# Loads, norms and fill work moved in the head of an attention and mixer kernel: channel weights in two late pieces, norms of pairs 6 to 8 ahead of the drain, rest rows last, more channel work in slots 6 to 8

## The chip, the cores and the metric

The kernel runs on one core of one Trainium2 chip. The metric is device time in microseconds (us). A profiled run gives a span that is about 1.8 us shorter than the run's own time (418.8 and 417.0 us for the kernel before).

The engines are called TensorE (PE in the profile; PEld is its weight load), VectorE (DVE), ScalarE (ACT), GpSimd (POOL) and SyncE (SP). In the traces each works through its own instructions in the order in which the kernel gives them.

## The reference

Cosine attention, then an MLP mixer over tokens and channels. All inputs and the output are float32; the kernel computes in float16 with float32 sums.

```python
# q, k, v: (8, 12, 448, 64); tau = 0.1
q_n = q / (norm(q, axis=-1) + 1e-6);  k_n = k / (norm(k, axis=-1) + 1e-6)
attn = softmax(q_n @ k_n.T / tau)
x = (attn @ v), heads side by side                 # (8, 448, 768)
xt = x.transpose(0, 2, 1)
u = x + (relu(xt @ w_tok1) @ w_tok2).transpose(0, 2, 1)      # token MLP, 448 -> 256 -> 448
out = u + relu(u @ w_ch1) @ w_ch2                            # channel MLP, 768 -> 1536 -> 768
```

## The kernel before

Two heads make a pair; there are 48 pairs, 6 for each batch. The order of instructions is written by hand in slots: slot i computes the scores of pair i, and beside them the values of pair i-1, the token MLP of pair i-2 and, from slot 6 on, some channel MLP of a finished batch. Slot 6 is special: it finishes the token MLP of pairs 4 and 5, the last two of the first batch (the "drain"), after which the first channel matmul can start. Three pairs make a half, which is the unit of loading and of the norms' tile of 45 columns (9 for the rest rows, 12 for each pair). The 448 rows are 3 blocks of 128 and 64 "rest rows". To get a pair ready takes a chain over four engines: squares (ScalarE, GpSimd), sums (VectorE), 1/norm by logarithms and exponentials (ScalarE), scaling to `kq` (GpSimd), transposes (TensorE) and a copy to `qk` (VectorE).

```python
def cast_v(n):                       # values of half n to float16
    (nc.vector if n < 3 else nc.gpsimd).tensor_copy(out=vts[n % NV]..., in_=vm[n]...)
    # ... rest rows of the values, GpSimd

def busy(n):                         # matmuls of the identity: keep TensorE active
    w = ps.tile([P, 512], FP32, name=f"busy_{n}", tag="b")
    for _ in range(n): nc.tensor.matmul(w..., id16[:], ..., start=True, stop=True)

def pv(p, a):                        # two row blocks of attn @ v
    # ...
    for mm in range(2):
        lo = P * (2 * a + mm)
        nc.tensor.matmul(psO[:, mm, :], pt[:, PX + lo:PX + lo + P], vx[:, j, 0:2 * E1], start=True, stop=False)   # rest rows
        for g in range(2):
            for c in range(NC):
                nc.tensor.matmul(psO[:, mm, E1 * g:E1 * (g + 1)], pt[:, at:at + P], vt[:, 2 * j + g, c, 0:E1],
                                 start=False, stop=(g == 1 and c == NC - 1))
    # ... reciprocal and x = psO * rec, VectorE

# --- tables: in which slot ---
early_sq = {3: 0, 4: 1, 5: 1, 6: 4, 7: 5, 8: 5, 9: 6, ...}            # squares of a pair
sum_at = at({p: s + 1 for p, s in sq_slot.items()})                    # sums one slot later
sc_at = at({p: {6: 5, 7: 6}.get(p, ...)})                              # scaling
cast_at = at({n: {1: 2, 2: 5}.get(n, 3 * n - 2) for n in range(1, NHALF)})

# --- before slot 0 ---
busy(26)
# ... squares, sums, norms of pair 0; scaled(0, nc.vector); rnorms(0, 0, 9)
sums(1)
scaled_x(0, nc.vector, 0, 1)         # pair 0's rest rows
rnorms(0, 21, 33)                    # pair 1's norms, ScalarE
# ...

# --- slot i ---
if i == FIRST:                       # FIRST = 6
    pv(i - 1, 0); m_tok1(i - 2); pv(i - 1, 1); next_qk(i); tok2(i - 2)
    m_tok1(i - 1); score(i, 0); tok2(i - 1); score(i, 1); feed(0.0, 3000.0)     # feed: channel units
elif i < NP_ALL:
    score(i, 0); score(i, 1)
# ... norm_sums, rnorms, norm_begin (squares), norm_scale by the tables
if i == 0:
    weights_ch1(0); weights_ch1(1)   # first channel weights, 2 x 1152 KB, issued by GpSimd
if i in (5, 6):
    weights_ch2(i - 5)               # second channel weights, 2 x 1152 KB
# ... values, scores of the rest, next pair's transposes, token MLP, channel units by quota
```

## Time and profile before

| | before |
|---|---|
| time, median of 3 runs (range) | 418.96 us (416.81 to 419.09) |
| span of the profiled run | 417.0 us |
| TensorE busy | 393.3 us, 94% |
| sum of TensorE's waits that the profile lists | 18.3 us, about 17 of them before 77 us |
| clock granted to TensorE | below 1.00 in most of 10 to 70 us, then 1.00 |

The table by stretches shows where TensorE is not full. The columns are the stretch, its length, then the busy time of PE, PEld, DVE, ACT and POOL (with instructions), the granted clock of TensorE, the share of the transfer engines, and GB/s.

```profile
10.00:20.00 10.00, 5.31 (x35) 2.62 (x35) 6.08 (x9) 7.26 (x17) 9.51 (x16) 0.63 1.15 260
20.00:30.00 10.00, 7.93 (x98) 5.32 (x96) 8.19 (x18) 8.62 (x19) 9.71 (x14) 0.86 1.19 225
30.00:40.00 10.00, 9.45 (x137) 6.76 (x136) 7.99 (x19) 7.29 (x11) 3.21 (x5) 1.00 1.14 230
40.00:50.00 10.00, 7.09 (x88) 5.52 (x84) 6.28 (x17) 4.05 (x9) 6.37 (x10) 0.83 1.19 276
50.00:60.00 10.00, 6.71 (x41) 3.15 (x40) 3.43 (x5) 6.36 (x13) 4.58 (x7) 0.84 1.25 224
60.00:70.00 10.00, 9.00 (x85) 4.91 (x83) 6.04 (x13) 7.58 (x18) 7.51 (x12) 0.81 1.10 214
70.00:80.00 10.00, 8.81 (x99) 5.43 (x99) 5.03 (x11) 6.98 (x14) 10.00 (x14) 1.00 0.92 211
```

A stretch with a granted clock below 1.00 is called cold here. From 80 to 400 us TensorE is busy 318.7 of 320 us at clock 1.00. The list of TensorE's waits names what it waited for (total us, times, longest):

```profile
PE psU L319 <- DVE r L303: 4.0, 4, 2.6
PE pst L240 <- DVE kq L218: 2.7, 1, 2.7
PE pst L240 <- POOL kq L207: 2.5, 2, 2.1
PE psS L259 <- DVE qk L245: 2.3, 3, 0.8
PE psS L259 <- ACT pt L260: 2.2, 6, 0.6
...
PE psG L347 <- DVE qk L245: 1.2, 1, 1.2
```

The longest wait of the first line, 2.6 us, is not slow VectorE work. VectorE's timeline around 41 us (start, duration, instruction, and in brackets the idle time before it and what ended it) shows the cast of the third half's values waiting for its load, and pair 3's relu `r` standing behind it in order. GpSimd's own wait for the rest keys of pair 6 is of the same kind: their load was late.

```profile
41.36 0.76 DVE L164 CAST vt<-vm 128x1152 f16<-128x1152 f32 x1 [1.14 <-DMA vm<-in_v_dram]
42.04 0.18 DVE L285 RECIPROCAL rec<-psO 128x4 f32<-128x4 f32 x1
42.25 0.42 DVE L286 TENSOR_TENSOR x<-psO,rec 128x256 f16<-128x256 f32 x1
42.59 0.41 DVE L303 TENSOR_SCALAR r<-psR 128x256 f16<-128x256 f32 x1
```

```profile
38.93 0.51 POOL L176 TENSOR_TENSOR sqx<-xk 128x192 f32<-128x192 f32 x1 [6.79 <-DMA xk<-in_k_dram]
...
55.42 0.82 POOL L207 TENSOR_TENSOR kq<-km,rn 128x384 f16<-128x384 f32 x1 [8.36 <-ACT rn L200]
```

The last of these lines is the second hole: GpSimd idles 8.36 us until ScalarE delivers norms, while TensorE waits for `kq` (the 2.5 us of the list):

```profile
56.30 0.34 PE L240 MATMUL pst<-id,kq 128*128 128x128 f16 x3 [2.09 <-POOL kq L207]
```

### The profile page before, as it was taken

The page shows a single profiled execution, that of the slowest core. Times are in us where ns is not written, and L with a number is a line of the kernel's source. Part 1 is how long each engine was busy: PE and PEld are TensorE (multiplying, and loading weights), DVE is VectorE, ACT ScalarE, POOL GpSimd, SP SyncE. Part 2 cuts the span into 40 slices and gives each one's busy share as a digit, 9 for nine tenths or more (in the row PEclk, how much of TensorE's full clock was granted, in tenths as well). Part 3 has the DMA queues.
Part 4 walks back from the last instruction along what each step waited for, and adds up shares of the span by engine and source line. Part 5 has one row for each costly group of instructions (what it writes and reads, how often), then busy time and mean ns, then how long its engine had stood idle before and what let it go on. Part 6 is the DMA issues. An engine that isn't in the chain of part 4 may idle for free.

```text
span 417.0 us, 9079 instructions
## 1 busy us (share of the span) xinstructions
PE 393.3 (94%) x3638; PEld 229.5 (55%) x3638; DVE 203.3 (49%) x456; ACT 225.6 (54%) x401; POOL 219.1 (53%) x321
## 2 busy tenths in 40 slices
PE   7588869899999999999999999999999999999995
PEld 3255634566655655555555655555555565565562
DVE  5687734657545464536553645446553443243021
ACT  4797367665376645674566445764576435521400
POOL 4993459999349293929392855839391600000000
PEclk9599879999999999999999999999999999999999
DMA  8999999946997396989897399989992353013012
GB/s 222 258 220 232 287 212 203 227 82 179 213 190 138 75 243 170 248 136 240 179 248 142 88 222 169 238 140 232 187 190 49 85 146 64 14 31 124 2 75 76
DMA packets 137162, 67.51 MB, mean 162 GB/s; under 512 B 93152, under 2 KB 133536, under 8 KB 137120
## 3 DMA queue, kind: packets, MB, share of 16 engines
q1 hardware_dynamic: 132800, 61.46, 68.6%
q0 software_dynamic: 3632, 5.18, 6.9%
q8 instruction: 28, 0.46, 0.5%
q10 hardware_dynamic: 688, 0.30, 0.2%
q14 instruction: 14, 0.11, 0.1%
HBM read 43.38 MB, written 11.01 MB: 130 GB/s over the span
## 4 chain that ended last, share of the span: by engine, by line
PE 79%; POOL 5%; DMA 4%; issue 4%; DVE 3%; ACT 2%; POOLq 0%
PE psF L361 25%; PE psG L347 24%; PE psO L281 7%; PE psS L259 7%; DMA vm<-in_v_dram 4%; PE psR L300 4%; PE psU L319 4%; PE psX L266 3%; PE psO L277 3%; POOL kq L207 2%; POOL sq L176 2%; POOL sqx L176 1%; ACT pt L260 1%; PE psU L324 1%; POOL kq L218 1%
## 5 line engine op out<-in xcount | busy, mean ns | idle before, releaser
L260 ACT ACTIVATE pt<-psS 128x896 f16<-128x896 f32 x144 | 126.5, 915 | 82.0 <-PE psS L259 81.9
L347 PE MATMUL psG<-ut,wc1t 128*128 128x448 f16 x576 | 123.3, 355 | 1.8 <-DVE qk L245 1.2
L361 PE MATMUL psF<-wc2t,gt 128*128 128x384 f16 x672 | 117.1, 326 | 0.0
L349 ACT ACTIVATE gt<-psG 128x448 f16<-128x448 f32 x96 | 52.3, 544 | 75.1 <-PE psG L347 75.0
L207 POOL TENSOR_TENSOR kq<-km,rn 128x384 f16<-128x384 f32 x47 | 39.6, 843 | 94.9 <-ACT rn L200 93.6
L361 PEld LDWEIGHTS <-gt 128*128 128x128 f16 x672 | 63.1, 98 | 41.3 <-issue 3.3
L347 PEld LDWEIGHTS <-wc1t 128*128 128x128 f16 x576 | 52.4, 98 | 49.6 <-issue 7.9
L364 DVE TENSOR_TENSOR ost<-psF,ur 128x384 f32<-128x384 f32 x56 | 31.2, 557 | 78.4 <-PE psF L361 75.0
L281 PE MATMUL psO<-vt,pt 128*128 128x65 f16 x1152 | 59.2, 196 | 0.0
L281 PEld LDWEIGHTS <-pt 128*128 128x128 f16 x1152 | 52.4, 99 | 5.2
L189 DVE TENSOR_REDUCE ssq<-sq 128x12 f32<-128x768 f32 x48 | 45.1, 948 | 14.3 <-POOL sq L176 14.2
L259 PE MATMUL psS<-qk 64*128 64x448 f16 x288 | 46.1, 367 | 4.7 <-DVE qk L245 2.3
L277 PE MATMUL psO<-vx,pt 128*128 128x130 f16 x192 | 43.0, 224 | 0.1
L286 DVE TENSOR_TENSOR x<-psO,rec 128x256 f16<-128x256 f32 x96 | 40.7, 424 | 3.3
L176 POOL TENSOR_TENSOR sq<-km 128x384 f32<-128x384 f32 x47 | 39.0, 833 | 5.4 <-DMA km<-in_k_dram 5.3
L285 DVE RECIPROCAL rec<-psO 128x4 f32<-128x4 f32 x96 | 17.1, 179 | 49.9 <-PE psO L281 49.6
L207 POOL TENSOR_TENSOR kq<-qm,rn 128x384 f16<-128x384 f32 x47 | 38.9, 827 | 0.0
L329 DVE TENSOR_TENSOR ut<-psU,xT 128x448 f16<-128x448 f32 (+2 forms) x39 | 17.6, 478 | 26.9 <-PE psU L319 18.3
L176 POOL TENSOR_TENSOR sq<-qm 128x384 f32<-128x384 f32 x36 | 29.6, 823 | 1.3 <-POOL kq L218 0.5
L319 PE MATMUL psU<-w2t,r 128*128 128x448 f16 x96 | 26.2, 356 | 4.1 <-DVE r L303 4.0
L300 PE MATMUL psR<-x,w1t 128*128 128x128 f16 x384 | 29.6, 221 | 0.0
L259 PEld LDWEIGHTS <-qk 64*128 64x128 f16 x288 | 11.0, 94 | 32.7 <-issue 27.4
(61 smaller groups left out, 327.9 us busy)
## 6 DMA issues: line engine op xcount, KB each, us to landing
vm<-in_v_dram SPq DMA_DIRECT2D x16, 576.0 KB, 7.4
out_dram<-ost SPq DMA_DIRECT2D x24, 384.0 KB, 2.7
qm<-in_q_dram SPq DMA_DIRECT2D x15, 576.0 KB, 5.1
km<-in_k_dram SPq DMA_DIRECT2D x15, 576.0 KB, 7.1
wc1t<-in_moe_w_ch_dram POOLq DMA_DIRECT2D x2, 1152.0 KB, 16.8
wc2t<-in_moe_w_ch_dram POOLq DMA_DIRECT2D x2, 1152.0 KB, 12.8
out_dram<-ost SPq DMA_DIRECT2D x8, 192.0 KB, 2.8
xq<-in_q_dram SPq DMA_DIRECT2D x7, 192.0 KB, 8.0
```

The lines of the kernel that those rows point to most:

```text
L176: eng.tensor_tensor(out=out, in0=src, in1=src, op=ALU.mult)
L189: nc.vector.tensor_reduce(out=ssqs[p // HP % 3][:, lo:lo + 12], in_=sq[p][:].rearrange("p a g e -> p (a g) e"), axis=AXX.X, op=ALU.add)
L207: eng.tensor_tensor(out=kqs[n % 2][:, j, a, 0:NC, :].rearrange("p c (g e) -> p g c e", g=2), in0=src, in1=_bcast_free(rn, E), op=ALU.mult)
L259: nc.tensor.matmul(psS[:, g, 0:S], qk[r, P * c:P * (c + 1)], qk[r, 512:512 + S], start=True, stop=True)
L260: nc.scalar.activation(out=pt[:, 2 * S * c:2 * S * (c + 1)].rearrange("p (g s) -> p g s", g=2), in_=psS[:, :, 0:S], func=AF.Exp, scale=inv ...
L277: nc.tensor.matmul(psO[:, mm, :], pt[:, PX + lo:PX + lo + P], vx[:, j, 0:2 * E1], start=True, stop=False)
L281: nc.tensor.matmul(psO[:, mm, E1 * g:E1 * (g + 1)], pt[:, at:at + P], vt[:, 2 * j + g, c, 0:E1], start=False, stop=(g == 1 and c == NC - 1))
L300: nc.tensor.matmul(psR[:, tt, :], w1t[:, m, tt * P:(tt + 1) * P], xs[p][:, m, :], start=(m == 0), stop=(m == NC))
L319: nc.tensor.matmul(psU[:], rs[p][:, tt, :], w2t[:, tt, lo:lo + S], start=(tt == 0), stop=by_dma and tt == TT - 1)
L347: nc.tensor.matmul(psG[:], wc1t[:, dt, ct * P:(ct + 1) * P], ut[:, dt, sp], start=(dt == 0), stop=(dt == DT - 1))
L349: nc.scalar.activation(out=gt[:, ct, sp], in_=psG[:], func=AF.Relu)
L361: nc.tensor.matmul(psF[:], gt[:, ct, lo:lo + P], wc2t[:, ct, dh * DH:(dh + 1) * DH], start=(ct == 0), stop=(ct == CT - 1))
```

## The change

Its intent: let the third half's loads pass before the channel weights; get pairs 6 to 8 scaled before the drain, so that the pairs behind it are ready; keep the clock up with more dummy matmuls; hand out channel work sooner. The diff, cut:

```diff
 def cast_v(n):
-    (nc.vector if n < 3 else nc.gpsimd).tensor_copy(...)
+    (nc.vector if n < 2 else nc.gpsimd).tensor_copy(...)
 # busy() may write into any tile; 4 more dummies inside pair 0's transposes, 2 before
 # the first score of slots 0 to 3
+            if p == 0 and (a, c) == (0, NC):
+                busy(w, 4)
+        busy(psS[:, 0, :], fill)                         # in score(p, c, fill=0)
 # pv: rest rows last
-            nc.tensor.matmul(psO[:, mm, :], pt[:, PX + lo:PX + lo + P], vx[:, j, 0:2 * E1], start=True, stop=False)
...
-                                     start=False, stop=(g == 1 and c == NC - 1))
+                                     start=(g == 0 and c == 0), stop=False)
+            nc.tensor.matmul(psO[:, mm, :], pt[:, PX + lo:PX + lo + P], vx[:, j, 0:2 * E1], start=False, stop=True)
 # tables
-    early_sq = {3: 0, 4: 1, 5: 1, 6: 4, 7: 5, 8: 5, ...
+    early_sq = {3: 0, 4: 1, 5: 1, 6: 3, 7: 4, 8: 5, ...
-    sum_at = at({p: s + 1 for p, s in sq_slot.items()})
+    sum_at = at({p: s + (p != 8) for p, s in sq_slot.items()})
     # one norm call for all 45 columns of half 2, at the end of slot 5
-    sc_at = at({p: {6: 5, 7: 6}.get(p, ...
+    sc_at = at({p: {6: 5, 7: 5}.get(p, ...
-    cast_at = at({n: {1: 2, 2: 5}.get(...
+    cast_at = at({n: {1: 2, 2: 6}.get(...
 # before slot 0
+        scaled_x(0, nc.vector, 0, 1)
         sums(1)
-        scaled_x(0, nc.vector, 0, 1)
 # slots
-            quota = max(sum(t for t, _ in queue) - 2000.0, 0.0) / left
+            quota = max(...) / (4 if FIRST <= i < FIRST + 3 else left)
     # slot 6: both value halves, tok1(4), tok2(4), tok1(5), tok2(5), 2 us of channel work,
     # then transposes of pair 6, its scores, 2 us of channel work
-                norm_begin(p, nc.scalar if p < 12 else nc.gpsimd, nc.gpsimd)
+                norm_begin(p, nc.scalar if p < 18 else nc.gpsimd, nc.gpsimd)
-            if i == 0:
-                weights_ch1(0)
-                weights_ch1(1)
+            if i in (2, 4):
+                weights_ch1(i // 4)
-            if i in (5, 6):
-                weights_ch2(i - 5)
+            if i in (6, 7):
+                weights_ch2(i - 6)
     # end of slot 5
+                if i == FIRST - 1:
+                    norm_sums(8)
+                    norm_rn()
+                    for p in sc_at[i]:
+                        norm_scale(p, nc.gpsimd)
```

## The prediction

> **What bounds the kernel now.** TensorE is busy 393.3 of 417.0 us (the page). By stretches it is full at clock 1.00 from 80 to 400 us; almost all loss lies in the first 77 us. There the waits of TensorE add up to about 16 us: 2.7 us for the first rest rows (VectorE, until 12.4), 2.6 us until 43.1 (relu queued in VectorE's order behind the value cast, whose load landed at 41.4), about 3.3 us around 56 to 58 us for pair 6's scaled q and k (GpSimd behind the norms), and many small ones. After each gap of 2 us or more the clock drops: seven transposes take 0.93 to 0.95 us at 16, 21 and 59 us but 0.55 us at 30 us. The Trainium skill, "TensorE: Matmul & The Clock Gate", Part 1, says an idle TensorE falls back to half clock until it has been busy a while; the trace agrees. Three cold stretches (12 to 23, 43 to 46.5, 56 to 63.7 us) cost an estimated 8 us.
>
> The loads are bandwidth bound: GB/s by stretch is 220 to 260 from 0 to 60 us. The two channel pieces, issued at 19.8 and 20.6 us (1152 KB each), stand in front of the third half's keys and values.
>
> **What changes.**
> 1. First-layer channel weights are issued in slots 2 and 4: 1.7 us of GpSimd issue leaves the busy start, and 2.4 MB leaves the way of half 2. Its rest keys (landed 38.9 us) should land near 27, its values (41.4) near 30. The 2.6 us wait and its cold stretch go.
> 2. Norms of pairs 6 to 8 finish in slot 5, so pair 6 is scaled at about 42 to 45 us instead of 55 to 58 and beyond. The gap near 56 goes.
> 3. Warm-up: rest rows before the second sum saves about 1 us at 12 us; 12 dummy matmuls are added (about 0.22 us each warm, 2.6 us), mostly in idle time.
> 4. Rest rows last: 14 matmuls as before, at most 1 us in all. By the skill's "PSUM — Partial Sum Buffer" the start flag clears a whole bank, so results hold.
> 5. Channel units in slots 6 to 8: moved.
> 6. Query squares of pairs 12 to 17 on ScalarE (about 0.42 us) instead of GpSimd (0.82).
>
> **On the critical path.** Slots 0 to 2 stay bound by ScalarE's exponentials and norms and by GpSimd (9.5 to 9.7 of 10 us busy), so warming gains about 1 us there. Slot 6 keeps some 3 to 4 us of VectorE waits. Slots 7 and 8 become ScalarE bound: exponentials 2.9, norms 1.1, squares 0.9, relus 0.5 to 1.4 us. So of about 24 us lost in the head I expect 7 to 9 back; full TensorE carries it to the end.
>
> **Predicted:** 411.0 us, 80% range 406.5 to 415.5. Faster by over 2%: 0.43; within 2%: 0.55; slower: 0.02.
>
> **Signs.** Right: no value-load wait near 41; first channel matmul near 44 us instead of 50; clock 1.00 in 30 to 60 us; pair 7's transposes near 52 instead of 59.5; full TensorE from about 70 us. Wrong: clock still 0.6 in 10 to 20 us.
>
> **What would make it wrong.** The clock staying cold through slot 6 despite the fill; rest keys of pair 6 landing late and blocking GpSimd ahead of pair 5; slots 7 and 8 less ScalarE bound than I think, or a shorter value group in the whole run (down to 406).

## The result

| | before | after |
|---|---|---|
| time, median | 419.02 us (4 runs) | 414.26 us (4 runs, 413.90 to 414.79) |
| ratio after to before | | 0.9896, 95% interval 0.9857 to 0.9935: within 2% |
| span of the profiled run | 417.0 us | 412.1 us |
| TensorE busy | 393.3 us | 391.2 us |
| clock granted, 10 to 20 / 20 to 30 / 30 to 60 us | 0.63 / 0.86 / 1.00, 0.83, 0.84 | 0.83 / 0.83 / 1.00 |

Ratios here and below are the mean time of one kernel's fast runs over that of the other's fast runs of the same rounds, so not quite the ratio of the medians quoted. The result is correct, as are those of all runs below. The time lies inside the range, 3.3 us above its centre: about 4.8 us of the 8.0 forecast came.

The same stretches of the kernel after:

```profile
10.00:20.00 10.00, 6.75 (x45) 2.77 (x44) 5.65 (x9) 7.26 (x17) 9.06 (x16) 0.83 1.14 267
20.00:30.00 10.00, 7.78 (x87) 4.82 (x88) 8.21 (x17) 7.55 (x18) 8.11 (x13) 0.83 1.18 233
30.00:40.00 10.00, 9.13 (x136) 6.48 (x133) 8.82 (x22) 7.96 (x13) 6.04 (x8) 1.00 1.25 235
40.00:50.00 10.00, 7.87 (x100) 5.42 (x100) 6.04 (x16) 4.01 (x9) 4.68 (x7) 1.00 1.16 213
50.00:60.00 10.00, 8.47 (x80) 4.48 (x79) 3.99 (x7) 8.26 (x17) 5.93 (x10) 1.00 1.16 251
60.00:70.00 10.00, 7.21 (x82) 4.27 (x79) 4.59 (x10) 7.62 (x17) 9.72 (x15) 1.00 1.22 171
70.00:80.00 10.00, 10.00 (x112) 6.00 (x110) 6.91 (x15) 8.36 (x18) 8.18 (x13) 1.00 1.14 252
```

The clock holds from 30 us on, and 70 to 80 us is now full. But the dummies count as busy, so 6.75 against 5.31 us in the first line is not progress. TensorE's waits:

```profile
PE psS L266 <- ACT pt L267: 4.6, 7, 1.3
PE psU L326 <- DVE r L310: 3.2, 4, 1.5
PE psS L266 <- DVE qk L251: 3.0, 4, 0.8
...
PE pst L246 <- POOL kq L218: 0.7, 1, 0.7
```

The wait for pair 7's `kq` is gone; its transposes start without one:

```profile
54.74 0.55 PE L246 MATMUL pst<-id,kq 128*128 128x128 f16 x7
```

The wait for the relu is 1.5 us at most instead of 2.6, and for another reason. The wait for ScalarE's exponentials has doubled, from 2.2 to 4.6 us.

Milestones on TensorE, from its timeline (start, us), show how the lead grows. "Units" are the channel matmul groups done by then, 1.14 us each at full clock:

| | before | after | forecast |
|---|---|---|---|
| first scores, slot 0 | 13.50 | 13.13 | |
| scores of slot 3 | 28.43 | 29.36 | 1 us earlier |
| scores of slot 5 | 37.43 | 38.48 | |
| first channel matmul | 50.04 (pair 6's transposes, two score groups done) | 47.67 (neither done) | 44 |
| transposes of pair 7 | 56.30 (3 units) | 54.74 (4 units) | |
| transposes of pair 8 | 59.48 (3 units) | 56.86 (4 units) | |
| transposes of pair 10 | 72.83 (6 units) | 72.52 (9 units) | |

In front of pair 10's transposes the lead is 0.31 us and 3 units, which is 0.31 + 3 x 1.14 = 3.7 us. The kernel before then waits another 1.16 us at 75.72, where the kernel after waits for nothing; 3.7 + 1.2 = 4.9 us is the difference of the two spans. Behind 80 us nothing is gained or lost.

So the opening loses 0.9 us, the loads and slot 6 turn that into a lead of 2.7 us at pair 7 (1.56 + 1.14), the missing cold stretch makes it 3.8 at pair 8, and slots 7 to 9 add nothing until the wait at 75.72.

One slip of the prediction has to be corrected: it counts the pairs wrongly by one. The transposes at 59.5 us that it calls pair 7's are pair 8's, so its "52 instead of 59.5" is to be read against 56.86, and that sign failed by almost 5 us. The scaling from 55 us on that it calls pair 6's is that of pairs 7 and 8; the kernel before had scaled pair 6 at 41.50. After the change GpSimd scales pair 6 at 45.17, 3.7 us later than before, and pair 7 at 48.69 instead of 55.42.

What the opening looks like on TensorE's timeline after:

```profile
22.68 0.36 PE L266 MATMUL psS<-qk 64*128 64x448 f16 x2 [0.84 <-DVE qk L251]
24.39 0.37 PE L266 MATMUL psS<-qk 64*128 64x448 f16 x2 [1.34 <-ACT pt L267]
...
26.47 0.95 PE L246 MATMUL pst<-id,kq 128*128 128x128 f16 x7
...
28.84 0.59 PE L232 MATMUL psS<-id 128*128 128x512 f16 x2
29.36 0.55 PE L266 MATMUL psS<-qk 64*128 64x448 f16 x4
```

The seven transposes take 0.95 us at 26.47, so the clock is down again, after waits of 0.84 and 1.34 us. They took 0.55 us at 20.12. ScalarE's second group of exponentials of slot 2 starts at 24.66 us instead of 24.13; that 0.5 us comes from pair 1's norms, which ScalarE began at 12.54 instead of 11.00 because their sum now stands behind the rest rows. The delay runs through GpSimd (pair 1 scaled at 13.82 instead of 13.11) and VectorE (pair 3's sum at 19.90 instead of 19.37) to ScalarE's next norms. The last two lines show two dummies taking 0.5 us right in front of scores that wait for nothing else.

What slot 6 looks like, first on VectorE, then on TensorE:

```profile
42.86 0.94 DVE L189 TENSOR_REDUCE ssq<-sq 128x12 f32<-128x768 f32 x1
43.72 0.17 DVE L292 RECIPROCAL rec<-psO 128x4 f32<-128x4 f32 x1
...
44.82 0.41 DVE L310 TENSOR_SCALAR r<-psR 128x256 f16<-128x256 f32 x1
```

```profile
45.29 0.55 PE L326 MATMUL psU<-w2t,r 128*128 128x448 f16 x2 [1.50 <-DVE r L310]
...
47.09 0.55 PE L326 MATMUL psU<-w2t,r 128*128 128x448 f16 x2 [0.60 <-DVE r L310]
...
47.67 2.43 PE L354 MATMUL psG<-ut,wc1t 128*128 128x448 f16 x12
```

Pair 8's sum (0.94 us) is issued at the end of slot 5 and stands in front of pair 5's values and pair 4's relu, for which the drain waits. GpSimd meanwhile has nothing to do until the one norm call for all 45 columns is through:

```profile
31.60 0.50 POOL L176 TENSOR_TENSOR sqx<-xk 128x192 f32<-128x192 f32 x1
...
45.17 0.83 POOL L207 TENSOR_TENSOR kq<-km,rn 128x384 f16<-128x384 f32 x1 [8.62 <-ACT rn L200]
```

The first of these two lines answers the 6.79 us wait of before: the rest keys of pair 6 are there, without a wait.

### The profile page after: what moved, and what is told of

It reads as the page before. It is cut to its first block, busy times and chain, and to the rows that moved or that the text cites. A ratio compares the mean times of both kernels' runs of the same rounds, so it can differ in the third digit from the quotient of the medians.

```text
span 412.1 us, 9121 instructions
## 1 busy us (share of the span) xinstructions
PE 391.2 (95%) x3650; PEld 226.4 (55%) x3650; DVE 201.6 (49%) x455; ACT 226.5 (55%) x405; POOL 213.0 (52%) x314
## 4 chain that ended last, share of the span: by engine, by line
PE 82%; DVE 6%; POOL 4%; ACT 3%; issue 2%; DMA 1%; POOLq 0%; DVEq 0%; ACTq 0%
PE psF L368 26%; PE psG L354 25%; PE psO L287 8%; PE psS L266 7%; PE psR L307 5%; PE psU L326 5%; PE psX L273 3%; PE psO L289 2%; ACT pt L267 1%; POOL kq L207 1%; DVE ssq L189 1%; DVE ssq L193 1%; POOL sq L176 1%; DVE x L293 1%; PE psU L331 1%
## 5 line engine op out<-in xcount | busy, mean ns | idle before, releaser
L287 PE MATMUL psO<-vt,pt 128*128 128x65 f16 x1152 | 57.8, 194 | 0.0
L266 PE MATMUL psS<-qk 64*128 64x448 f16 x288 | 45.1, 359 | 7.8 <-ACT pt L267 4.6
L289 PE MATMUL psO<-vx,pt 128*128 128x130 f16 x192 | 42.0, 219 | 0.0
L336 DVE TENSOR_TENSOR ut<-psU,xT 128x448 f16<-128x448 f32 (+2 forms) x39 | 17.6, 478 | 21.4 <-PE psU L326 15.9
L274 ACT ACTIVATE pt<-psX 128x448 f16<-128x448 f32 x48 | 26.1, 543 | 0.0
```

Source lines behind the costliest of these rows:

```text
L266: nc.tensor.matmul(psS[:, g, 0:S], qk[r, P * c:P * (c + 1)], qk[r, 512:512 + S], start=True, stop=True)
```

## The experiments

Each took the changed kernel with one part undone, unless said otherwise. The kernel before ran 11 times beside each of the four sets: medians 419.21 (set 1), 418.13 (set 2), 418.92 (set 3) and 418.25 us (set 4). The changed kernel was not run again beside them, and the sets ran on three chips (6, 0, 6 and 1), so ratios compare better than medians. The changed kernel's is 0.9896 (0.9857 to 0.9935); the interval of e10 lies clear above it, those of v2 and v3 lie clear below, and all others overlap with it. Three theories of the opening were on trial: A, the moved rest rows alone cost it; B, the dummies cost it; C, the two together do.

### Set 1: the opening and the weights

**e1_sum_first**: pair 1's sum ahead of the rest rows again.

```diff
-        scaled_x(0, nc.vector, 0, 1)
         sums(1)
+        scaled_x(0, nc.vector, 0, 1)
```

> The changed kernel with VectorE's order in the opening put back: the second sum of squares (pair 1) before pair 0's rest rows. Theory A (the reorder delays pair 1's norms, and through GpSimd and ScalarE the whole opening: in the changed kernel pair 1's norms start at 12.5 us instead of 11.0 and the scores of slot 3 at 29.4 us instead of 28.4): pair 1's norms start near 11 us, slot 3's scores at 28.4 to 28.9 us, time 0.5 to 1.0 us below the changed kernel's 414.3. Rival B (the dummy matmuls and the cold clock make the loss): slot 3's scores stay at 29.2 us or later, time within 0.3 us of the changed kernel.

Measured: 414.15 us median, ratio 0.9868 (0.9831 to 0.9905). Slot 3's scores start at 29.16 us, 0.2 before those of the changed kernel; slot 2's transposes again take 0.95 us. A alone falls.

**e2_no_fill**: without the 12 added dummies.

```diff
-                busy(w, 4)
+                pass
-                score(i, 0, 2 if i < 4 else 0)
+                score(i, 0, 0)
```

> The changed kernel without its 12 added dummy matmuls (4 inside pair 0's transposes, 2 before each of the first four scores); the 26 of the start stay. Rival B (the dummies stand in front of scores that are ready: 0.5 us in slot 3): slot 3's scores 0.5 us earlier than 29.4, time 0.3 to 0.8 us below 414.3. If instead the dummies earn their place by holding the clock: cold stretches grow beyond the present two (9.5 to 18.6 and 25 to 28.3 us) and the time rises by 0.5 to 2 us. Theory A expects neither: within 0.5 us, since ScalarE and GpSimd set the pace there.

Measured: 416.21 us median (413.73 to 417.75), ratio 0.9908 (0.9865 to 0.9951). The clock is 0.64 and 0.68 in the two stretches from 10 to 30 us, and slot 3's scores start at 29.33: what the missing dummies save, a longer cold stretch (26.35 to 30 us) takes. It is not faster, so B alone falls too. By the median it is 2.0 us slower, which is the second case of the expectation (the dummies hold the clock), but the six runs spread over 4 us, the intervals of the ratios overlap, and v3 below does not repeat it.

**e3_weights_early**: the first channel weights back in slot 0.

```diff
+            if i == 0:
+                weights_ch1(0)
+                weights_ch1(1)
-            if i in (2, 4):
-                weights_ch1(i // 4)
```

> The changed kernel with both channel-weight pieces issued in slot 0 again, as before; all else as changed. If the late issue is what makes the earlier norms possible: GpSimd waits for pair 6's rest keys until about 38 us, and as that square now stands ahead of pair 5's scaling in its order, TensorE stalls in slot 4 for 4 us or more; time 418 to 424 us, no better than the kernel before. Rival (the loads had slack once the value cast moved to slot 6): within 1.5 us of 414.3.

Measured: 415.96 us median, ratio 0.9894 (0.984 to 0.9948): 1.7 us slower than the changed kernel by the medians, while the ratios do not tell the two apart; the expected stall of 4 us or more in slot 4 and the 418 us or more did not come. GpSimd did wait again for pair 6's rest keys, 3.69 us, but finished scaling pair 5 at 36.8, before TensorE asked at 37.75. In the profile, which is of the slowest of the four runs, the loss arose earlier: the issue of the two loads, about 0.9 us each, stands in GpSimd's busy opening, and slot 3's scores start at 30.89 instead of 29.36. In that profile the late weights are worth their issue time more than the load that they let pass. The load of the third half's values took 20.3 us from issue to landing (18.1 in the kernel before), and still TensorE has no wait near 41 us: its cast now stands on GpSimd in slot 6, at 54.9 us. So inside the changed kernel the moved cast alone takes that wait away.

**e5_before_late_weights**: the kernel before with only the weights in slots 2 and 4.

```diff
-            if i == 0:
-                weights_ch1(0)
-                weights_ch1(1)
+            if i in (2, 4):
+                weights_ch1(i // 4)
```

> The kernel before with one thing changed: the two channel-weight pieces issued in slots 2 and 4. If the value-load wait at 41 us and the cold clock after it were the main loss, and pair 6's gap merely shifts along with the stream: no wait at 41 us, first channel matmul near 46 us instead of 50, time 414 to 415.5 us, most of the whole change's gain. If the gap near 56 us is set by the norms alone (rival): the 2.6 us are given back there, first channel matmul earlier but pair 7's transposes still near 59 us, time 417.5 to 419.

Measured: 416.71 us median, ratio 0.9923 (0.9885 to 0.9962). So this part alone is worth about 2.5 us (1.6 to 4.8 by the interval), between the two cases of the expectation. The 2.6 us wait near 41 us is 1.0: VectorE no longer waits for the load, but the cast (0.95 us at 38.90) still stands in front of the relu. The first channel matmul starts at 47.13, earlier than in the changed kernel, and slot 3's scores at 27.61. Then the old hole is there again: pair 7's transposes wait 2.09 and 0.45 us at 53.39, and the clock is 0.70 in 50 to 60 us.

### Set 2: the opening undone, the value order, the quota, and a better slot 6

**e9_sum_first_no_fill**: both edits of e1 and e2.

> The changed kernel with both parts of the opening undone: pair 1's sum before pair 0's rest rows, and none of the 12 added dummies. Undone one at a time they gave nothing (scores of slot 3 at 29.2 and 29.3 us), while the kernel before with only the late weights had them at 27.6. Theory C (the two parts do the same harm: either makes TensorE wait 1.3 us for ScalarE in slot 2, the clock falls at 25 us, and the stretch where TensorE sets the pace is run cold): slot 3's scores at 27.5 to 28.0 us, seven transposes of slot 2 in 0.55 us, first channel matmul near 46 us instead of 47.7, time 1.0 to 2.0 us below the changed kernel's 414.3 if no later cold stretch comes. Rival D (something else in the changed kernel, such as pair 6's square on GpSimd ahead of pair 5's scaling, or the order of the value matmuls): slot 3 again at 29 us, time within 0.5 us.

Measured: 414.13 us median (413.85 to 418.87), ratio 0.9925 (0.9886 to 0.9963). This is the opening of before without the weights' issue. In its profile the clock stayed down until 27.9 us:

```profile
20.00:30.00 10.00, 9.33 (x99) 5.86 (x96) 8.55 (x19) 8.63 (x19) 7.60 (x12) 0.62 1.15 236
```

Even so, slot 3's scores start at 28.54 and pair 10's transposes at 71.70 with 9 units, 0.8 us ahead of the changed kernel. The span is 412.4, not shorter: in 90 to 400 us TensorE is busy 307.6 us where the changed kernel has 308.7, so the lead seems to have gone in small waits later. C is not confirmed by the time.

Over all profiles the start of slot 3 sorts by the opening. With the sum first and no dummies it is 28.43 (before), 28.54 (e9), 27.61 (e5), 27.43 (v1, below) and 27.56 (v2). With dummies, with the rest rows first, or with both it is 28.98 to 29.74, and 30.89 in e3. So the edits of the opening do delay the head by about a microsecond. But the same opening (e5, v1, v2 and e9, which differ in it only by the order of the value matmuls and by the work for later pairs) came up to full clock at 23.9, 21, 22.6 and 27.9 us, so much of a single profile is chance.

**e4_rest_first**: the old order of the value matmuls.

```diff
+            nc.tensor.matmul(psO[:, mm, :], pt[:, PX + lo:PX + lo + P], vx[:, j, 0:2 * E1], start=True, stop=False)
-                                     start=(g == 0 and c == 0), stop=False)
-            nc.tensor.matmul(psO[:, mm, :], pt[:, PX + lo:PX + lo + P], vx[:, j, 0:2 * E1], start=False, stop=True)
+                                     start=False, stop=(g == 1 and c == NC - 1))
```

> The changed kernel with the value matmuls in the order of before (rest rows first). If the order matters only in the opening, where the rest rows' exponential comes last: within 0.4 us of the changed kernel, a group of 14 value matmuls 0.50 us as before. If weight loads behind the short matmuls cost in each of the 96 groups: 1 to 2 us slower, the groups in the full stretch visibly longer than 0.50 us.

Measured: 414.09 us median, ratio 0.9906 (0.988 to 0.9931). The order is neutral in time. That it is right at all agrees with the Trainium skill, "PSUM — Partial Sum Buffer", "The four PSUM rules": the first matmul with the start flag clears the written marks of a whole 2 KiB bank, and a later matmul overwrites where the mark is clear and adds where it is set. Both orders gave correct results. (The prediction's "clears a whole bank" is to be read so: the marks, not the data.)

**e6_quota**: the old quota of channel work.

```diff
-            quota = max(...) / (4 if FIRST <= i < FIRST + 3 else left)
+            quota = max(...) / left
```

> The changed kernel with the old quota of channel units in slots 7 and 8 (the queue spread over all slots left); slot 6's own order stays as changed. If ScalarE's exponentials, norms and relus and GpSimd's scaling set the pace of slots 7 and 8, so that channel units there only fill TensorE's gaps: one or two units fewer before slot 9's transposes, which come no or hardly earlier, and 1 to 2 us slower. If TensorE set the pace there: slot 9's transposes earlier by 1.1 us for each unit moved, time within 0.3 us.

Measured: 413.20 us median, ratio 0.9884 (0.986 to 0.9909). Pair 10's transposes start at 69.94 with 6 units instead of 72.52 with 9: 2.6 us earlier for 3.4 us of channel work less. All three units lie in slot 8 behind pair 9's transposes, and there each unit less brought pair 10's transposes 1.0 of its 1.14 us forward (9.11 us in the changed kernel against 6.14). That is the second case of the expectation: in this part of slot 8 TensorE set the pace, not ScalarE. The expected loss of 1 to 2 us did not come, and the median is 1.1 us below that of the changed kernel, which the overlapping intervals leave open. That TensorE is fed sooner bought nothing.

**v1_norms_slot5**: a version meant to be better. The opening of before; pair 6's norms at the end of slot 4 and its scaling in slot 5, where GpSimd idled 8.6 us; pair 9's squares in slot 5 too; pair 8's sum behind the first relu of slot 6, and the slot's order as follows.

```diff
                 pv(i - 1, 0)
-                pv(i - 1, 1)
                 m_tok1(i - 2)
+                pv(i - 1, 1)
+                next_qk(i)
                 tok2(i - 2)
                 m_tok1(i - 1)
-                tok2(i - 1)
-                feed(0.0, 2000.0)
-                next_qk(i)
+                norm_sums(8)
                 score(i, 0)
+                rnorms(2, 21, 45)
+                norm_scale(7, nc.gpsimd); norm_scale(8, nc.gpsimd)
+                tok2(i - 1)
+                norm_sums(9)
                 score(i, 1)
-                feed(0.0, 2000.0)
+                rnorms(3, 0, 21)
+                norm_scale(9, nc.gpsimd)
+                feed(0.0, 4000.0)
```

> A version meant to beat both: the opening of the kernel before; pair 6 scaled in slot 5 from its own norms, on GpSimd, idle from 36.5 to 45 us in the changed kernel; the value cast of pairs 6 to 8 there too; pair 8's sum after the relu of pair 5 instead of ahead of pair 5's value results; pair 9's squares and norms in slots 5 and 6; slot 6 with pair 6's transposes and scores between the token matmuls, as before the change. If the serial VectorE chain of slot 6 (two waits of 1.5 and 0.6 us and the copies) and ScalarE's wait for pair 9 to 11's norms (2.3 us at 64 us) are what the changed kernel still loses: no TensorE wait over 0.8 us from 30 to 75 us, pair 7's transposes near 52 us instead of 54.7, TensorE full from about 62 us, time 408 to 411 us. If ScalarE's total work in slots 5 to 8 is the bound: pair 7's transposes earlier, but slot 9's no more than 1.5 us earlier than 72.5, time 412 to 414.

Measured: 413.00 us median (411.01 to 415.40), ratio 0.9878 (0.984 to 0.9916). The head did what was wanted: first channel matmul at 45.03, pair 7's transposes at 50.17, pair 10's at 64.63 with 9 units, 7.9 us ahead of the changed kernel. Then the queries of the sixth half were not there. ScalarE's and TensorE's timelines:

```profile
76.87 0.52 ACT L174 ACTIVATE sq<-qm 128x384 f32<-128x384 f32 x1 [4.07 <-DMA qm<-in_q_dram]
```

```profile
78.28 0.35 PE L287 MATMUL psO<-vt,pt 128*128 128x65 f16 x6 [3.54 <-ACT gt L356]
```

SyncE's queue shows why: the load of those queries was issued at 70.67 us, behind two transposes that held the queue from 61.67 for 8.89 us, and the two pieces of the second channel weights, issued at 52.70 and 57.00, took 12 to 17 us to land in the same stretch. A lead in the head was handed to the next load.

### Set 3: the norms, and the loads moved

**e10_norms_late**: squares, sums, norms and scaling of pairs 6 to 8 in the slots of before, with all the rest of the change in place.

```diff
-    early_sq = {... 6: 3, 7: 4, 8: 5, ...
+    early_sq = {... 6: 4, 7: 5, 8: 5, ...
-    sum_at = at({p: s + (p != 8) for p, s in sq_slot.items()})
+    sum_at = at({p: s + 1 for p, s in sq_slot.items()})
-    sc_at = at({p: {6: 5, 7: 5}.get(p, ...
+    sc_at = at({p: {6: 5, 7: 6}.get(p, ...
     # norms of half 2 in two calls again; block at the end of slot 5 removed
```

> The changed kernel with the norms of pairs 6 to 8 put back to slots 4 to 6 (squares of 6 and 7 one slot later, sums and norms of 7 and 8 in slot 6 behind the first channel units, pair 7 scaled in slot 6); late weights, dummies, slot 6's own order and the quota as changed. If the earlier norms carry their part: pair 7's scaling stands behind the relus of slot 6 as in the kernel before, TensorE waits 2 us or more ahead of pair 7's transposes and runs cold behind it, pair 7's transposes at 57 to 58 us instead of 54.7, time 1.5 to 3 us above the changed kernel's 414.1 to 414.3. If the late weights made all the gain (416.7 alone against 419.2 in the same rounds) and the rest is noise: within 0.7 us.

Measured: 419.80 us median, ratio 1.0024 (0.9984 to 1.0064). The whole gain is gone, 5.5 us by the medians, where 1.5 to 3 were expected. GpSimd's line for pair 7's scaling and ScalarE's for its norms:

```profile
56.85 0.83 POOL L207 TENSOR_TENSOR kq<-km,rn 128x384 f16<-128x384 f32 x1 [11.49 <-ACT rn L200]
```

```profile
55.10 0.54 ACT L356 ACTIVATE gt<-psG 128x448 f16<-128x448 f32 x1 [0.40 <-PE psG L354]
55.54 0.31 ACT L197 ACTIVATE rn<-ssq,tiny 128x24 f32<-128x24 f32 x1
```

The norms stand on ScalarE behind the relus of the channel units, which the new slot 6 feeds first. TensorE waits 2.5 us for pair 7, and the clock is 0.69 in 60 to 70 us. So the new order of slot 6 gains nothing without the early norms, and the two were tested only together; v1 and v2 have early norms with another order and do better. This run also shows slot 6 without pair 8's sum in front of the relu:

```profile
46.04 0.55 PE L326 MATMUL psU<-w2t,r 128*128 128x448 f16 x2 [0.68 <-DVE r L310]
```

The wait is 0.68 instead of 1.50 us; the second one is 0.60 as before.

**v2_loads_later**: v1 with the old quota, the second piece of the second channel weights in slot 8 instead of 7, and the squares of pairs 15 and 17 a slot later.

```diff
-    early_sq = {... 15: 10, 16: 11, 17: 11}
+    early_sq = {... 15: 11, 16: 11, 17: 12}
-            if i in (6, 7):
-                weights_ch2(i - 6)
+            if i in (6, 8):
+                weights_ch2(i // 2 - 3)
```

> The version of slots 5 and 6 from the last runs, with its new wait taken away. There ScalarE stood 4.1 us at 73 us on the load of pair 15's queries, TensorE 3.5 us behind it, and the clock fell: the load was issued at 70.7 us, behind both second-layer weight pieces (issued 52.7 and 57.0 us). Here the second piece is issued in slot 8 instead of 7, pair 15's squares stand one slot later (pair 17's too), and the channel quota is the old one, which cost nothing when put back. If that wait was all that v1 lost again: TensorE full from about 57 us to the end, span near 406, time 406.5 to 409 us. If the loads bind as a whole at that point (all of 50 to 75 us at 200 to 230 GB/s): another wait of 2 us or more turns up between 60 and 90 us and the time is 410 to 413.

Measured: 406.82 us median (406.07 to 408.46), ratio 0.9719 (0.9686 to 0.9752). It beats both kernels by over 7 us. Stretches and waits:

```profile
40.00:50.00 10.00, 9.69 (x100) 5.96 (x97) 6.92 (x14) 6.53 (x18) 7.32 (x12) 1.00 1.18 211
50.00:60.00 10.00, 9.18 (x105) 5.48 (x104) 5.60 (x12) 9.39 (x18) 7.47 (x12) 1.00 1.21 248
60.00:70.00 10.00, 9.77 (x119) 6.00 (x116) 7.30 (x15) 9.52 (x20) 9.84 (x15) 1.00 1.25 206
```

```profile
PE psS L266 <- ACT pt L267: 2.8, 8, 0.8
PE pst L246 <- DVE kq L218: 2.7, 1, 2.7
```

The 2.7 us of the second line are the opening, as before the change. From 40 to 70 us TensorE is busy 28.6 of 30 us, against 23.6 in the changed kernel. What took v1's wait away can be read from ScalarE's timeline:

```profile
76.72 0.54 ACT L174 ACTIVATE sq<-qm 128x384 f32<-128x384 f32 x1
```

The queries were issued at 64.38 instead of 70.67 us but took 11.3 instead of 6.1, so they landed at 75.7, only 1.1 us earlier. ScalarE comes to their square at 76.72, after other work, where v1 stood idle for 4.07 us: the square moved by a slot hides the load. The three edits were not tried one by one.

**v3_with_dummies**: v2 with the 12 dummies (the edit of e2 the other way).

> The version before this one with the change's 12 dummy matmuls. Theory: the dummies do not save time on the average but make the clock's course in the opening the same in every run (all profiles with them: warm at about 18.6 us, cold again 25 to 28.3 us; without them the clock rose at 21, 23, 24 and 28 us): the six times lie within 1.5 us of each other where the version without them spreads over 3 us or more, the median within 1 us of it. Rival (they save time): the median 1 us or more below it; rival (they cost time): above it by 0.8 us or more.

Measured: 407.04 us median (406.20 to 409.15), ratio 0.9724 (0.9686 to 0.9761). Slot 3 starts at 28.98 in its profile, against 27.56, but the medians are 0.2 us apart. A guess, that dummies narrow the spread between runs, has no support here either: 3.0 us with them, 2.4 without.

### Set 4: the squares

**e7_squares**: the query squares of pairs 12 to 17 on GpSimd again.

```diff
-                norm_begin(p, nc.scalar if p < 18 else nc.gpsimd, nc.gpsimd)
+                norm_begin(p, nc.scalar if p < 12 else nc.gpsimd, nc.gpsimd)
```

> The changed kernel with only one part undone: the query squares of pairs 12 to 17 are back on GpSimd (0.82 us each) instead of ScalarE (0.46 each). Theory: this part is neutral, because TensorE is full from about 68 us on and these squares start in slot 8, at about 63 us or later; then the median is within 1 us of the changed kernel's (414.3), the ratio to the kernel before is 0.986 to 0.992, and TensorE's share of 70 to 90 us stays 10.0 of 10. Rival: it relieves GpSimd, the slower of the two helpers around slots 8 to 11 (9.72 of 10 us busy in 60 to 70 us), so that undoing it brings waits of TensorE for scaled q and k or for the exponentials behind them, 1 to 3 us in all between 63 and 90 us, and a median of 415.5 to 417.

Measured: 414.86 us median (413.89 to 419.45), ratio 0.9935 (0.9892 to 0.9977). The ratio is a little above the expected band because of the one run at 419.45; the median is inside it. From 63 to 90 us TensorE waits as in the changed kernel (0.74, 0.48 and 0.53 us) and is 10.00 of 10 busy in 70 to 90 us, while GpSimd goes from 8.18 to 9.93 busy in 70 to 80 us. The part takes work off GpSimd and leaves the time alone.

## Why the prediction was right or wrong

- **The bound.** Right: the loss lay in the first 77 us, and full TensorE carried the head's gain unchanged to the end (3.7 us plus a wait of 1.2 us gone, against 4.9 us in the span). The gain was 4.8 us where 8.0 were forecast; that the time lies inside the stated range owes much to the width of that range, 9 us.
- **Late weights.** Right as a mechanism: the third half's values took 9.1 us from issue to landing instead of 18.1 and its rest keys 8.6 instead of 17.6, the waits on both went, and the part alone gives about 2.5 us (e5). A share of it is not the transfer but the two issues leaving GpSimd's opening (27.61 against 28.43 for slot 3 in e5, and e3's profile). And in the changed kernel the wait on the values would have gone without it, by the moved cast (e3).
- **Early norms.** Right that the gap near 56 us goes, though it was pair 7's and not pair 6's. Without them the changed kernel is no faster than the kernel before (e10), but that undoes them under an order of slot 6 made for them, so what they are worth alone is not shown.
- **"Warming gains about 1 us there" and "rest rows before the second sum saves about 1 us"**: wrong, the first mis-sized term. The first scores came 0.37 us earlier, but slot 3 started 0.93 us later. The clock did rise earlier (0.83 instead of 0.63 in 10 to 20 us), in a stretch where TensorE waits for ScalarE, and where a fast clock mostly lengthens the wait (1.34 us at 24.39). In those waits it fell again, and the cold matmuls came where TensorE sets the pace. The reordering put pair 1's norms 1.5 us later on ScalarE. For slot 3 the forecast was 1 us earlier and the profile has 0.93 later, so the term is about 1.9 us off. What that is worth in the final time stays open: undoing both edits brought the head 0.8 us forward but not the time (e9), and the dummies make 0.2 us in v2.
- **"First channel matmul near 44"**: wrong, the second mis-sized term; it was 47.67. The number did not follow from the prediction's own terms: slot 6 took 5.55 us from its first value matmul (42.12) to the first channel matmul, of which 2.1 were the waits that the prediction itself had put at 3 to 4. The start can be estimated at about 40 us (44.05 in the kernel before, less the wait of 2.6 us, some 0.4 us of cold matmuls and the 1 us forecast for the opening); from there 44 left no room for the waits. 42.12 instead of about 40 is the lost opening. About 0.8 of the 2.1 us are due to pair 8's sum in front on VectorE: without it the two waits are 0.68 and 0.60 us (e10). In v2, with that sum behind the relu, slot 6 does more (pair 6's transposes and two score groups as well) in 4.9 us (40.27 to 45.17).
- **Slots 7 and 8 ScalarE bound**: right in part. Two waits are new: 1.04 us at 61.71 for exponentials, and 0.74 at 63.25 for rest keys that GpSimd scaled after waiting 4.01 us for ScalarE's norms. They offset what the kernel before lost there by running partly cold, so that the lead at pair 8 (3.8 us) was no larger at pair 10 (3.7). But behind them TensorE set the pace in slot 8 (e6).
- **Rest rows last, squares on ScalarE**: right, neutral (e4, e7).
- **Clock.** The two signs that concern it came: 1.00 in 30 to 60 us, full TensorE from about 70. The Trainium skill, "TensorE: Matmul & The Clock Gate", Part 1, on which the prediction leaned, says an idle TensorE falls to half clock. The trace agrees in kind (seven transposes 0.95 us cold, 0.55 warm), but a warm clock was worth less than the prediction had it, as it came at the wrong place.

The parts do not add up to a list: e5 gives 2.5 us and e10 says that the rest without the early norms takes that away again. What is shown is that the late weights help the kernel before (e5), that the changed kernel has no gain without the early norms (e10), and that undoing value order, quota or squares loses no time clear of noise. The value cast moved to GpSimd was not tried by itself.

## What to carry to other kernels

Look for the stretch in which another engine idles before a serial part (here GpSimd, 8.6 us) and move the preparation of what follows into it; then read, for each in-order engine, what stands in front of the instruction that the serial part waits for. A faster clock pays only where TensorE sets the pace, and the dummy matmuls, most of them in a stretch paced by ScalarE, changed no time clear of noise: the median without them was 2.0 us higher in the changed kernel (e2) and 0.2 lower in v2. In the profile the two in front of ready scores took 0.5 us. When the head gets faster, check the loads of the next stage and where their first reader stands in its engine's order: v1 lost most of its lead of 7.9 us to one late load. A weight load moved by a slot and two squares moved by one (with the old quota) turned it into the fastest version; the load came only 1.1 us earlier by it, so by the trace most of the wait went because its reader moved.

## What the Trainium skill lacked or had wrong

- "TensorE: Matmul & The Clock Gate", Part 1, has the clock fall after at least one idle window of about 3.4 us. Here it fell at about 24.9 us with waits of only 0.84 and 1.34 us in the 3 us before. So two waits that leave TensorE idle for 2.2 of about 3 us were enough here, which the table of the two states does not say. The same part, under its second failure mode, says in kind that many short idle times between groups of matmuls make the clock go up and down, but gives no length for them.
- The same part says that the moment of warming varies from run to run. This agrees: 21, 22.6, 23.9 and 27.9 us for the same opening. It also puts the cost of the warming under 1% of a typical kernel; slot 3's start moved by 1.1 us among these four, 0.3% of the span, which agrees, but is as large as some of the effects that one wants to tell apart.
- The same page, Part 4, says that the full clock does not engage for transposes. Here seven transposes, which the profile shows as matmuls with the identity, took 0.95 us in cold and 0.55 us in warm stretches, so they do run faster when the clock is up. Whether transposes by themselves bring it up, no run here shows.
